# Four wo heads behind the cache stream, zero fills on ScalarE, MLP output in four partial sums, and TensorE's tail as a guarded last trip of its loop, in a one-core decode kernel

## The chip, the cores and the metric

Each kernel runs on one NeuronCore of a Trainium2 chip. The metric is device time in microseconds; "same" means within 2%. One execution of each kernel is profiled; the span on a profile page runs from the first to the last instruction, and the timed number is about 2 us above it.

## The reference

A decode step: attention over a K/V cache of 8192 positions (batch 4, 8 K/V heads, two query heads for each, head size 256), gated by the SiLU of an MLP.

```python
xn = layernorm(x)                                   # [4, 1, 448]
q  = xn @ wq                                        # 16 heads of 256
p  = softmax(q k^T * 256**-0.5)                     # k_cache [4, 8, 8192, 256], two q heads per k head
s  = (p v) @ wo                                     # v_cache [4, 8, 8192, 256], wo [4096, 448]
xn2 = layernorm(xn)
b  = xn + gelu(xn2 @ w3) @ w4                       # the rest of the MLP block is zero for S == 1
out = x + s * silu(b)
```

The caches are 268 MB of the 279 MB that must be read. There are 32 pairs of batch and K/V head; "K of head 2" below is the K cache (4 MiB) of the third pair in the order of work.

## The kernel before

SyncE issues every load, in order, on one queue. K and V have two buffers each.

```python
sp.dma_start(wq); sp.dma_start(w3); sp.dma_start(w4)        # into the two V buffers
load_k(0); load_k(1)
sp.dma_start(wo_sb[...], A_wo...).then_inc(S["dwo"], 16)    # all 16 heads, 3.5 MiB
for h in range(2, NH):
    load_k(h)            # waits until K of head h-2 has been transposed  (v_k)
    load_v(h - 2)        # waits until PV of head h-4 is done             (v_v)
load_v(NH - 2); load_v(NH - 1)                              # the last V in four pieces
```

```python
with nc.Fori(0, NH // 2, engines=[PE], head_slot={PE: 0}):
    body(0); body(1)
h = NH - 1
take(pe, "dwo", 16)
...                                        # wo of K/V heads 0 to 6, PV of head 30
for i in range(NPIECE):                    # V of head 31, piece by piece as it lands
    take(pe, "dvl%d" % i, 16)
    ... matmul(pst[1 + dh][:, 0:PVW], kn[...V piece...], pT[...])
take(pe, "v_ot")                           # VectorE scales the result
f_o(HKV - 1).then_inc(S["p_o"], 1)         # wo of the last K/V head: 16 matmuls
```

Then VectorE forms the output in two instructions and SyncE and ScalarE store it. The MLP output is 56 matmuls of 112 columns into one sum; GpSimd fills the parts of the V buffers that hold no weights with zeros (2,048 and 3,840 columns), because the first two passes of PV, both in the loop's first trip, multiply them by zero.

Of the kernel before, what the change touches and what calls it, by code (L numbers as in the profile page):

```python
# [32 lines left out]
def bass_recurrent_scan__gqa_block_cached__mixer_s_mlp__decode_kernel(  # L33
# [29 lines left out]
    assert D == NQD * DQ and Bn <= PQ  # L63
# [14 lines left out]
    CGW = P // NCG  # L78
    PV_PARTS = (0, 8, 16, 28, NCH)
    J_BC, J_TR, J_SUM = 1, 3, 8  # L80
    PVW = 32
    PIECES = (0, 32, 48, 56, NCH)
    NPIECE = len(PIECES) - 1

    x2d = A_x.rearrange("b s d -> b (s d)")
    out2d = out.rearrange("b s d -> b (s d)")

    with ExitStack() as es:
        def sb(name, shape, dty):
# [12 lines left out]
        OT = sb("OT", [P, HKV, REP, NHALF, Bn], BF16)  # L102
# [5 lines left out]
        sel = sb("sel", [P, REP], F32)  # L108
        po = sb("po", [P, DH], F32)
# [15 lines left out]
        xn4 = sb("xn4", [P, DQ], F32)  # L125
        res = sb("res", [P, DQ], F32)
# [3 lines left out]
        sg = sb("sg", [P, DQ], F32)  # L130
# [10 lines left out]
            + ["dvl%d" % i for i in range(NPIECE)]  # L141
            + ["p_td", "p_ta", "p_sc", "p_m1", "p_m2", "p_m3", "p_tr", "p_pv", "p_x", "p_q", "p_h", "p_h2", "p_o"]
            + ["v_ev", "a_ev", "v_rmax", "v_diag", "v_neg", "v_ot", "a_exp", "g_q", "g_c",
               "v_s", "v_k", "v_v", "v_po", "v_o", "g_o", "g_p", "g_f", "v_xT", "v_qT", "v_hT", "v_bout", "v_c", "v_w", "a_c", "v_out"])}
# [11 lines left out]
        q_ps = pst[1]  # L156
        h_ps = pst[2]
        h2_ps = pst[3]
        o_ps = pst[0]

# [7 lines left out]
        def prog_sp(sp):  # L168
# [10 lines left out]
            def load_k(h):  # L179
                b, g = divmod(h, HKV)  # L180
                if h >= 2:
                    sp.wait_ge(S["v_k"], h - 1)
                sp.dma_start(kn_dst(h), A_k_cache[b, g].rearrange("(p c) d -> p (c d)", p=P)
                             ).then_inc(S["dk%d" % (h % 2)], 16)

            def load_v(h):
                b, g = divmod(h, HKV)
# [5 lines left out]
                else:  # L193

                    sp.wait_ge(S["v_k"], h)
                    for i in range(NPIECE):
# [8 lines left out]
            sp.dma_start(wo_sb[:, :, :, :].rearrange("p h c n -> p h (c n)"),  # L205
                         A_wo.rearrange("(h p c) n -> p h (c n)", p=P, c=NHALF)
                         ).then_inc(S["dwo"], 16)
# [4 lines left out]
            load_v(NH - 1)  # L212
            sp.wait_ge(S["v_out"], 1)
# [6 lines left out]

        def prog_pool(gp):
            def put(h):
                b, g = divmod(h, HKV)
                gp.wait_ge(S["v_o"], h + 4)
                gp.tensor_copy(OT[:, g, :, :, b],
                               otmp[:, h % 2].rearrange("p dh r -> p r dh")
                               ).then_inc(S["g_p"], 1)
                gp.wait_ge(S["g_p"], h + 1)
                gp.sem_inc(S["g_o"], 1)
# [4 lines left out]
            c(gp.memset(ones_f[:, :], 1.0))  # L234
            c(gp.memset(pT[:, :, :].rearrange("p s n -> p (s n)"), 0.0))
            c(gp.memset(vflat[1][:, DK * HDH:NCH * DH], 0.0))
            c(gp.memset(vflat[0][:, DK * FH + NF * D:NCH * DH], 0.0))
            c(gp.memset(diag[:, :], 0.0))
            c(gp.memset(po[:, :], 0.0))
            c(gp.memset(rz[:, :, :].rearrange("p s r -> p (s r)"), 1.0))  # L240
            c.sync()
            for t in (ident_b, ident_f):
                c(gp.affine_select(out=t[:, :], in_=t[:, :], compare_op=ALU.not_equal, fill=1.0,  # L243
                                   base=0, pattern=[[-1, P]], channel_multiplier=1))
            gp.wait_ge(S["v_qT"], 1)
            for h in range(NH):
                b, g = divmod(h, HKV)
# [19 lines left out]
        def prog_act(act):  # L267
            act.dma_start(x_sb[:, :], x2d).then_inc(S["dx"], 16)
            c = _Chain(act, S["a_c"])
            for k, col in ((1, 0), (2, 8)):  # L270
                act.wait_ge(S["v_w"], k)
                c(act.activation(st[:, col + 2:col + 3], st[:, col + 1:col + 2], ACT.Sqrt))
            act.wait_ge(S["v_w"], 3)
            c(act.activation(gel_b[:, :], gel_a[:, :], ACT.Tanh))
            act.wait_ge(S["v_w"], 4)
            c(act.activation(sg[:, :], bout[:, :], ACT.Tanh, scale=0.5))
# [25 lines left out]
        def prog_dve(v):  # L302
# [34 lines left out]
            c(v.memset(psc[1][:, 0:NCH * REP], 0.0))  # L337
            c(v.memset(psv[:, 0:DH], 0.0))
            c.sync()
            v.sem_inc(S["v_diag"], 1)  # L340
            v.sem_inc(S["v_po"], 1)
            v.sem_inc(S["g_o"], 5)
            v.sem_inc(S["dv0"], 16)
            v.sem_inc(S["dv1"], 16)
            c(v.memset(h2_ps[:, 0:DQ], 0.0))
            for t in (x4, xn4):
                c(v.memset(t[:, :], 0.0))
# [7 lines left out]
            v.wait_ge(S["g_c"], 11)  # L355
            idv = ident_f[:, :].rearrange("p (m t) -> p t m", t=NHF)
            c(v.tensor_reduce(par[:, :], idv, AX.X, ALU.add))
            c(v.tensor_reduce(sel[:, :], ident_f[:, :].rearrange(
                "p (j r) -> p r j", j=NCG)[:, 0:REP], AX.X, ALU.add))
            c.sync()  # L360
            for k, dst in ((0, xnT), (1, xn2T)):
                v.wait_ge(S["p_x"], k + 1)

                for t in range(NHF):
                    for a in range(NHF):
# [3 lines left out]
                ins.then_inc(S["v_xT"], 1)  # L369
            v.wait_ge(S["p_q"], 1)  # L370
            c(v.tensor_copy(qT[:].rearrange("p b g dh hh -> p (b g dh hh)"),
                            q_ps[:, 0:NKC * Bn]))
            c.sync()
            v.sem_inc(S["v_qT"], 1)
# [10 lines left out]
            v.wait_ge(S["a_c"], 3)  # L385
# [5 lines left out]
            for src, dst in ((x_f, x4), (xn_f, xn4)):  # L391
                for i in range(NQD):
                    c(v.tensor_copy(dst[i * PQ:i * PQ + Bn, :], src[:, i * DQ:(i + 1) * DQ]))
            c.sync()
            v.wait_ge(S["p_h2"], 1)
            c(v.tensor_tensor(bout[:, :], h2_ps[:, 0:DQ], xn4[:, :], ALU.add))
            c.sync()
            v.sem_inc(S["v_w"], 1)
            v.sem_inc(S["v_bout"], 1)
            v.wait_ge(S["a_c"], 4)  # L400
            c(v.tensor_scalar(sg[:, :], sg[:, :], 1.0, 0.5, op0=ALU.add, op1=ALU.mult))
            c.sync()
            c(v.tensor_tensor(sg[:, :], sg[:, :], bout[:, :], ALU.mult))
# [18 lines left out]
            def f_rz(h):  # L422
                take(v, "p_m3")
                v.reciprocal(rz[:, h % 2, :], psm[:, P + REP:P + 2 * REP]
                             ).then_inc(S["v_s"], 1)
                take(v, "v_s")

            def f_po(h):
                take(v, "p_pv")
                v.sem_inc(S["v_v"], 1)  # L430
                v.tensor_copy(po[:, :], psv[:, 0:DH]).then_inc(S["v_po"], 1)  # L431

            ot_src = psv[:, DH:DH + NHALF * REP].rearrange("p (a r) -> p a r", a=NHALF)

            def f_ot(h, last=False):
                b, g = divmod(h, HKV)
                take(v, "p_tr")
                if not last:
                    take(v, "g_o")
# [5 lines left out]
                v.sem_inc(S["v_ot"], 1)  # L445
                v.sem_inc(S["v_o"], 1)

            with nc.Fori(0, NH // 2, engines=[mybir.EngineType.DVE]):
                for h in range(2):
                    for j in range(NGR):  # L450
# [4 lines left out]
                        if j == J_TR + 1:  # L455
                            f_ot(h - 3)
                        if j == J_SUM + 2:
                            f_rz(h - 1)
# [5 lines left out]
            f_negb(h)  # L464
            f_ot(h - 2, True)
            f_rz(h)
            f_po(h - 1)
            f_ot(h - 1, True)
            b, g = divmod(h, HKV)
            take(v, "p_pv")  # L470
            for dh in range(NHALF):
                ins = v.tensor_tensor(OT[:, g, :, dh, b], pst[1 + dh][:, 0:REP],
                                      rz[:, h % 2, :], ALU.mult)
            ins.then_inc(S["v_ot"], 1)
            v.wait_ge(S["p_o"], 1)
            c(v.tensor_tensor(res[:, :], o_ps[:, 0:DQ], sg[:, :], ALU.mult))  # L476
# [4 lines left out]
        def prog_pe(pe, xn_mark, xn2_mark):  # L481
            pe.wait_ge(S["g_c"], 11)
            for k, (src, mark) in enumerate(((xn_b, xn_mark), (xn2_b, xn2_mark))):
# [6 lines left out]
                if k == 0:  # L490
                    take(pe, "v_xT")
            take(pe, "dwq", 16)
            qo = q_ps[:, 0:NKC * Bn].rearrange("p (b a g dh hh) -> p g hh dh a b", b=Bn, a=NHF,
                                               dh=NHALF, hh=REP)
            for c in range(NQC):
                g, r = divmod(c, REP * NHALF)
                hh, dh = divmod(r, NHALF)
                for j in range(DK):
                    ins = pe.matmul(qo[:, g, hh, dh], wq_sb[:, j, c * P:(c + 1) * P],
                                    xnT[:, j], start=(j == 0), stop=(j == DK - 1))  # L500
# [8 lines left out]
            ins.then_inc(S["p_h"], 1)  # L509
            take(pe, "dw4", 16)  # L510
            take(pe, "v_hT")
            for k in range(NFK):
                for a in range(NHF):
                    for i in range(NQD):
                        ins = pe.matmul(h2_ps[i * PQ:i * PQ + Bn, 0:DQ], hT[:, k, a, :],
                                        w4_sb[:, a, k, i * DQ:(i + 1) * DQ],
                                        start=(k == 0 and a == 0),
                                        stop=(k == NFK - 1 and a == NHF - 1))
            ins.then_inc(S["p_h2"], 1)
            take(pe, "v_bout")  # L520
# [34 lines left out]
            def f_sum(h):  # L555
                take(pe, "a_exp")
                pe.matmul(psm[:, P + REP:P + 2 * REP], ones_f[:, :], rowsum[:, h % 2, :],  # L557
                          start=True, stop=True).then_inc(S["p_m3"], 1)

            def f_pv(h, lo, hi):  # L560
                if lo == 0:
                    take(pe, "v_ot")
                    take(pe, "dv%d" % (h % 2), 16)
                for kk in range(lo, hi):
                    o = kk % NCG * CGW
                    ins = pe.matmul(psv[o:o + REP, 0:DH],  # L566
                                    pT[:, h % 2, kk * REP:(kk + 1) * REP], vb[:, h % 2, kk, :],
                                    start=(kk < NCG), stop=(kk >= NCH - NCG))
                if hi == NCH:
                    ins.then_inc(S["p_pv"], 1)  # L570

            def f_tr(h):
                take(pe, "v_po")
                for dh in range(NHALF):
# [113 lines left out]
```

## Time and profile before

| | before |
|---|---|
| time, median of 3 runs | 660.26 us (659.96 to 661.8) |
| span of the profiled run | 658.7 us |
| bytes read | 279 MB |
| rate, 80 to 640 us | 428 to 436 GB/s in every 20 us |
| last bytes of the last V piece land | 654.15 us |
| output stores issued | 656.61 us |

These are lines of the page of the kernel before: the span; the rate of the loads in 40 equal slices of the span; the instruction queue (packets, MB, share of the DMA engines); and TensorE's transposes (count, then busy time, mean ns of one, idle time before them).

```profile
span 658.7 us, 25245 instructions
...
GB/s 363 433 410 427 427 432 430 434 434 430 432 432 430 432 434 430 434 432 434 428 434 428 432 432 436 430 432 436 426 434 430 436 430 434 434 426 436 426 426 223
...
q8 instruction: 10, 0.16, 0.1%
...
L528 PE MATMUL pst<-ident_b,kn 128*128 128x128 bf16 x4096 | 345.5, 238 | 101.2 <-PEq L219 99.7
```

The rate is flat but for the first and last slices: the kernel is its load stream. TensorE sat idle for 101 us ahead of the transposes, waiting for K. So nothing inside the loop can pay unless it keeps loads from being issued. Every 20 us window from 80 to 640 us reads 428 to 436 GB/s; whether a higher rate was to be had is not shown.

The timeline of SyncE (start us, issue us, what), kernel before:

```profile
43.85 0.33 SPq L183 DMA_DIRECT2D kn<-in_A_k_cache_dram  x1
51.57 0.33 SPq L191 DMA_DIRECT2D vb<-in_A_v_cache_dram  x1
64.95 0.33 SPq L183 DMA_DIRECT2D kn<-in_A_k_cache_dram  x1
71.49 0.33 SPq L191 DMA_DIRECT2D vb<-in_A_v_cache_dram  x1
82.61 0.33 SPq L183 DMA_DIRECT2D kn<-in_A_k_cache_dram  x1
86.54 0.33 SPq L191 DMA_DIRECT2D vb<-in_A_v_cache_dram  x1
```

These are K of head 2, V of head 0, K of head 3, V of head 1, K of head 4, V of head 2. A load adds 16 to its semaphore, and the trace has the time of each of the 16 increments, taken here as one for each of the core's 16 DMA engines. wo, ahead of K of head 2 in the queue, completes from 47.79 (first engine) to 50.23 (last): K of head 2 was issued 4 us before the first engine ran dry. V of head 1 completes from 86.71 to 89.07. From then on each 4 MiB follows the one before by 9.71 us.

The windows view (window, its length, then busy us and instruction count of PE, PEld, DVE, ACT and POOL, the granted TensorE clock, DMA share and GB/s), kernel before:

```profile
core 0: us, PE busy (x) PEld busy (x) DVE busy (x) ACT busy (x) POOL busy (x), PEclk, DMA share, GB/s
...
80.00:84.00 4.00, 4.00 (x108) 3.41 (x105) 2.11 (x5) 1.98 (x2) 0.00 (x0) 1.00 1.01 434
84.00:88.00 4.00, 3.95 (x91) 3.29 (x84) 2.04 (x6) 1.02 (x1) 0.19 (x1) 1.00 1.01 434
88.00:92.00 4.00, 4.00 (x96) 4.00 (x94) 2.05 (x6) 3.38 (x7) 0.00 (x0) 1.00 1.03 442
```

The end of TensorE's first trip, kernel before, from its timeline (start us, busy us, engine, line, operation, count, and in brackets the idle before it):

```profile
70.36 0.37 PE L548 MATMUL psm<-ident_f,rmax 128*2 128x128 f32 x1
70.52 1.91 PE L528 MATMUL pst<-ident_b,kn 128*128 128x128 bf16 x16
```

The last instruction of the trip and the first of the next follow each other. The end of the kernel before, from the timeline of all engines (start us, busy us, engine, line, operation, count, and in brackets the idle before it):

```profile
654.29 0.59 PE L630 MATMUL pst<-pT,kn 128*128 128x32 bf16 x16 [0.62 <-PEq L219]
655.03 0.23 DVE L472 TENSOR_TENSOR OT<-pst,rz 128x2 bf16<-128x2 f32 x2 [6.84 <-DVEq L219]
...
655.40 0.55 PE L610 MATMUL pst<-wo_sb,OT 128*4 128x112 bf16 x16 [0.53 <-PEq L219]
656.00 0.28 DVE L476 TENSOR_TENSOR res<-pst,sg 128x112 f32<-128x112 f32 x1 [0.74 <-PE pst L610]
656.31 0.28 DVE L478 TENSOR_TENSOR out_b<-res,x 128x112 bf16<-128x112 f32 x1
656.61 0.69 SPq L165 DMA_DIRECT2D out_dram<-out_b  x2
```

From the landing of the last V piece (654.15) to the store (656.61) is 2.46 us of strictly serial work.

### The profile page before, as it was taken

How to read it: one execution, taken by the hardware profiler on the slowest of the kernel's cores; microseconds unless marked ns; L12 is line 12 of the kernel's file. 1: busy time of each engine (PE TensorE's matmuls, PEld its weight loads, DVE VectorE, ACT ScalarE, POOL GpSimd, SP SyncE). 2: the span in 40 equal slices, each digit the busy share in tenths (PEclk: the TensorE clock that was granted, in tenths of full speed). 3: DMA queues.
4: the chain of work that ended last, by engine and by line, in shares of the span. 5: the costliest groups of instructions: out<-in, count | busy, mean ns of one | idle time of the engine just before them, and what ended most of it. 6: DMA issues, size and time to landing. Idle time of an engine off the chain costs nothing. (4 is left out here: it accounts for less than half of the span.)

```text
span 658.7 us, 25245 instructions
## 1 busy us (share of the span) xinstructions
PE 531.3 (81%) x11091; PEld 481.5 (73%) x11091; DVE 260.7 (40%) x585; ACT 252.6 (38%) x362; POOL 17.0 (3%) x76
## 2 busy tenths in 40 slices
PE   1489999896979879678887867987969698867895
PEld 1378888885969778577777756877858688866784
DVE  7234455242433424343433434442524343433440
ACT  1044444451434435234443423443524344423340
POOL 4000000000000000000000000000000000000000
PEclk9988799696797969798987979896979896978996
DMA  8999999999999999999999999999999999999995
GB/s 363 433 410 427 427 432 430 434 434 430 432 432 430 432 434 430 434 432 434 428 434 428 432 432 436 430 432 436 426 434 430 436 430 434 434 426 436 426 426 223
DMA packets 12324, 279.18 MB, mean 424 GB/s; under 512 B 1172, under 2 KB 3224, under 8 KB 3736
## 3 DMA queue, kind: packets, MB, share of 16 engines
q1 hardware_dynamic: 12288, 278.99, 98.9%
q8 instruction: 10, 0.16, 0.1%
q14 instruction: 2, 0.02, 0.0%
q10 hardware_dynamic: 24, 0.01, 0.0%
HBM read 278.99 MB, written 0.00 MB: 424 GB/s over the span
## 5 line engine op out<-in xcount | busy, mean ns | idle before, releaser
L528 PE MATMUL pst<-ident_b,kn 128*128 128x128 bf16 x4096 | 345.5, 238 | 101.2 <-PEq L219 99.7
L265 ACT ACTIVATE kT<-pst 128x1024 bf16<-128x1024 bf16 x224 | 229.4, 1024 | 361.7 <-ACTq L219 361.1
L528 PEld LDWEIGHTS pst<-ident_b,kn 128*128 128x128 bf16 x4096 | 277.6, 108 | 106.4 <-issue 105.8
L263 DVE COPY kT<-pst 128x1024 bf16<-128x1024 bf16 x288 | 197.8, 692 | 282.5 <-DVEq L219 282.3
L540 PE MATMUL psc<-qc,kT 128*128 128x2 bf16 x4096 | 179.2, 165 | 0.7 <-issue 0.7
L540 PEld LDWEIGHTS psc<-qc,kT 128*128 128x128 bf16 x4096 | 158.8, 98 | 22.8 <-issue 22.8
L566 PE MATMUL psv<-vb,pT 128*2 128x256 bf16 x2112 | 84.8, 284 | 2.5 <-issue 1.8
L566 PEld LDWEIGHTS psv<-vb,pT 128*2 128x2 bf16 x2112 | 39.8, 84 | 10.9 <-issue 2.8
L407 DVE TENSOR_REDUCE rmax<-psc 128x2 f32<-128x128 f32 x32 | 9.3, 292 | 49.4 <-DVEq L219 49.4
L576 PE MATMUL psv<-sel,po 128*128 128x2 f32 x136 | 25.1, 289 | 0.7 <-PEq L219 0.6
L576 PEld LDWEIGHTS psv<-sel,po 128*128 128x128 f32 x136 | 23.0, 237 | 0.9 <-issue 0.9
L284 ACT ACTIVATE pT<-psc,negb 128x64 bf16<-128x64 f32 x66 | 20.6, 332 | 5.2 <-ACTq L219 5.2
L412 DVE TENSOR_REDUCE gmax<-psm 2x1 f32<-2x128 f32 x32 | 8.9, 279 | 33.9 <-DVEq L219 33.9
L250 POOL COPY qc<-qT 128x4 bf16<-128x4 bf16 x32 | 5.9, 187 | 584.1 <-DVEq L430 574.5
L552 PEld LDWEIGHTS psm<-diag,ones_f 2*128 2x128 f32 x66 | 12.7, 239 | 6.0 <-issue 4.6
L552 PE MATMUL psm<-diag,ones_f 2*128 2x2 f32 x66 | 15.4, 301 | 1.1 <-PEq L219 0.9
L431 DVE COPY po<-psv 128x256 f32<-128x256 f32 x33 | 14.0, 425 | 4.8 <-DVEq L219 4.1
L284 ACT ACTIVATION_READ_ACCUMULATOR pT<-psc,negb 128x1 f32 x66 | 13.6, 206 | 0.0
L557 PE MATMUL psm<-rowsum,ones_f 128*128 128x2 f32 x66 | 12.4, 257 | 0.0
L486 PE MATMUL pst<-ident_b,xn_b 4*128 4x4 bf16 x14 | 0.6, 161 | 13.5 <-DVE xn_b L333 8.8
L486 PEld LDWEIGHTS pst<-ident_b,xn_b 4*128 4x128 bf16 x14 | 0.5, 100 | 13.6 <-POOL ident_f L243 8.8
L557 PEld LDWEIGHTS psm<-rowsum,ones_f 128*128 128x128 f32 x66 | 10.3, 196 | 0.2 <-issue 0.2
(77 smaller groups left out, 97.1 us busy)
## 6 DMA issues: line engine op xcount, KB each, us to landing
kn<-in_A_k_cache_dram SPq DMA_DIRECT2D x32, 4096.0 KB, 26.0
vb<-in_A_v_cache_dram SPq DMA_DIRECT2D x31, 4096.0 KB, 31.7
vb<-in_A_wq_dram SPq DMA_DIRECT2D x1, 3584.0 KB, 11.3
wo_sb<-in_A_wo_dram SPq DMA_DIRECT2D x1, 3584.0 KB, 46.9
vb<-in_B_w_dram SPq DMA_DIRECT2D x2, 1568.0 KB, 16.3
kn<-in_A_v_cache_dram SPq DMA_DIRECT2D x1, 2048.0 KB, 27.1
kn<-in_A_v_cache_dram SPq DMA_DIRECT2D x1, 1024.0 KB, 29.1
kn<-in_A_v_cache_dram SPq DMA_DIRECT2D x2, 512.0 KB, 30.2
```

Source lines behind the costliest of these rows:

```text
L263: engine.tensor_copy(dst, src).then_inc(S["v_ev"], 1)
L265: engine.activation(dst, src, ACT.Copy).then_inc(S["a_ev"], 1)
L284: ins = act.activation(pv_p[:, :, hh], sc[:, :, hh], ACT.Exp, bias=negb[:, s, hh:hh + 1], scale=SCALE, accum_out=rowsum[:, s, hh:hh + 1])
L407: v.tensor_reduce(rmax[:, :], psc[h % 2][:, 0:NCH * REP].rearrange("p (k h) -> p h k", h=REP), AX.X, ALU.max).then_inc(S["v_rmax"], 1)
L412: v.tensor_reduce(gmax[:, :], psm[0:REP, 0:P], AX.X, ALU.max).then_inc(S["v_s"], 1)
L431: v.tensor_copy(po[:, :], psv[:, 0:DH]).then_inc(S["v_po"], 1)
L528: ins = pe.transpose(dst[:, t * P:(t + 1) * P], kn[:, h % 2, GC * j + kl, half * P:(half + 1) * P], ident_b[:, :])
L540: ins = pe.matmul(psc[h % 2][:, kk * REP:(kk + 1) * REP], kT[:, j % RING, t * P:(t + 1) * P], qc[:, h % 2, half, :], start=(half == 0), st ...
L552: pe.matmul(psm[:, P:P + REP], ones_f[0:REP, :], diag[:, :], start=True, stop=True).then_inc(S["p_m2"], 1)
L557: pe.matmul(psm[:, P + REP:P + 2 * REP], ones_f[:, :], rowsum[:, h % 2, :], start=True, stop=True).then_inc(S["p_m3"], 1)
L566: ins = pe.matmul(psv[o:o + REP, 0:DH], pT[:, h % 2, kk * REP:(kk + 1) * REP], vb[:, h % 2, kk, :], start=(kk < NCG), stop=(kk >= NCH - NCG))
L576: ins = pe.matmul(psv[:, o:o + REP], po[:, dh:DH:NHALF], sel[:, :], start=True, stop=True)
```

## The change

Its intent: shorten that serial end by letting four heads of wo, which need no further attention work, land last; keep the code of the end from being fetched at the end, by making it a guarded last trip of the loop; and make the head of the program smaller and less dependent on GpSimd. The diff, cut to its core:

```diff
-            sp.dma_start(wo_sb[:, :, :, :]...).then_inc(S["dwo"], 16)
+            load_wo(NLATE, HQ, "dwo")                       # 12 heads; LATE = ((0, 1), (2,), (3,))
             for h in range(2, NH): load_k(h); load_v(h - 2)
             load_v(NH - 2); load_v(NH - 1)
+            for i, hs in enumerate(LATE):
+                load_wo(hs[0], hs[-1] + 1, "dwl%d" % i)     # 2 + 1 + 1 heads end the stream
 ... zero fills of the V buffers
-            c(gp.memset(vflat[1][:, DK * HDH:NCH * DH], 0.0))
-            c(gp.memset(vflat[0][:, DK * FH + NF * D:NCH * DH], 0.0))
+            for t in (vflat[1][:, DK * HDH:NCH * DH], vflat[0][:, DK * FH + NF * D:NCH * DH]):
+                c(act.activation(t, pT[:, 0, 0:1].broadcast_to([P, t.shape[1]]), ACT.Copy))
 ... MLP output; q and PV are widened in the same way (28 for 112, and 32 for 64 a head)
-                    for i in range(NQD):
-                        ins = pe.matmul(h2_ps[i * PQ:i * PQ + Bn, 0:DQ], hT[:, k, a, :],
-                                        w4_sb[:, a, k, i * DQ:(i + 1) * DQ], ...)
+                    o = i % NCG * CGW
+                    ins = pe.matmul(h2_ps[o:o + Bn, 0:D], hT[:, k, a, :], w4_sb[:, a, k, :], ...)
+            ...                                             # a copy, then four f32 matmuls add the sums
 ... TensorE's loop
-            with nc.Fori(0, NH // 2, engines=[PE], head_slot={PE: 0}):
-                body(0); body(1)
-            ...the tail...
+            with nc.Fori(0, NH // 2 + 1, engines=[e], head_slot={e: 64}) as it:
+                with pe.If(it != NH // 2):
+                    body(0)
+                    body(1)
+                with pe.If(it == NH // 2):
+                    finish()                                # the tail, ends with f_o of the late heads
```

The tail is rewritten too: wo of the early heads and the first pieces of the last V go into four partial sums each. The order of the batches is also reversed, and in a head the transposition of PV's result moves to the place of the row sums.

## The prediction

> **What bounds the kernel now.** The load stream: 429 to 436 GB/s in every 20 us stretch from 80 to 640 us (windows view); 279.2 MB at 434 GB/s is 643 of the 658.7 us span. TensorE waits 105 us for K (waits view), so compute inside the loop is worth nothing. What is left is the start and the end. The timeline's end: TensorE starts on the last V piece at 654.29 (0.59 us), VectorE scales until 655.26, 16 wo matmuls run 655.40 to 655.95, VectorE works until 656.59, the store lasts to 658.7.

> The last landing itself is late. By the trace's completion increments 15 of the 16 DMA engines finish the last V piece between 650.31 and 652.40, the sixteenth at 654.15. The instruction queue has a 16 KiB packet of 1.07 us at 644.15, just before one engine falls 1.8 us behind. [...] The code after the loop is fetched then, through the same DMA engines.

> **What the change does.**
> 1. Four of 16 wo heads (0.92 MB, about 2.3 us at the 385 GB/s of the wo load) move behind V. The bytes stay; V lands 2.3 us earlier, so its chain runs under the wo transfer. After the last landing 8 matmuls remain, about 0.3 us at the half clock of the tail (16 took 0.55). On the critical path: 1.66 us become 0.3; 1.3 us saved.
> 2. The tail becomes the loop's last trip, and TensorE's program shrinks from about 2530 to 1920 instructions (counted in the builds). All from the loop on should be fetched in the first trip, nothing at the end. Then the straggler goes and the stream ends near 652, not 654.15: 1.5 to 2 us saved.
> 3. Zero fills: 1.8 + 3.6 us of GpSimd become about 6 us of ScalarE (1024 columns take 1.02 us) between 10 and 17 us, before the Tanh at 20.9. Not critical: K of head 0 lands at 30.83.
> 4. q in 28 wide matmuls, not 112; MLP output in 14, not 56; PV in 32, not 64. The head is done at 24 us and waits for K anyway. Worth nothing.
> 5. Loop entry at slot 64 moves the fetch stalls of the first trip (2.1 us at 43.8, 1.5 at 59.4, 0.65 at 67.5). They matter only through the issue of the next loads. With wo shorter the queue runs dry 2.3 us earlier, near 45.5 on the fastest engine; K of head 2 was issued at 43.85, K of head 3 at 64.95, just in time. I expect at most a short dip on the faster engines, costing 0 to 0.7 us.

> **Predicted:** -1.3 - 1.8 + 0.2, about -3 us: 657.3 us, 8 in 10 between 655.6 and 659.4. Faster by over 2%: 0.01; within 2%: 0.98; slower: 0.01.

> **Signs.** Last V piece read near 650 to 651, last wo landing near 652 with increments within 2.2 us; no instruction packet after 100 us; store issued near 653.5; span near 655.7; loop stretches still 429 to 436 GB/s.

> **What would make it wrong.** The tail is fetched at the end after all [...]; starvation between 45 and 90 us above 1 us; TensorE at half clock is not through the other wo matmuls before the last landing; the straggler has another cause.

-1.3 - 1.8 + 0.2 is -2.8 us, its "about -3". The trace of the kernel before does show the packets: eight of 16 KiB from 20.43 to 72.22 us, none through the later trips of the loop, then two, at 644.15 and 651.46. The "half clock of the tail" is a granted clock of 0.50 from 650 us to the end.

## The result, and the profile after

| | before | after |
|---|---|---|
| time, median | 660.24 us (4 runs) | 660.73 us (4 runs, 660.33 to 661.85) |
| ratio, 95% interval | | 1.0005 (0.9985 to 1.0025), same |
| span of the profiled run | 658.7 us | 658.8 us |

A ratio is the mean time of one kernel's fast runs over that of the other's fast runs of the same rounds, so it is not quite the ratio of the medians. The expected 3 us did not come.

The page after, the same lines:

```profile
span 658.8 us, 22917 instructions
...
GB/s 363 441 382 424 432 366 444 418 444 430 430 444 416 446 414 446 424 436 440 420 442 418 444 418 442 436 426 440 420 444 416 444 428 434 434 426 442 418 429 296
...
q8 instruction: 7, 0.11, 0.1%
```

The last slice is fuller (296 for 223), as intended. But the third and the sixth slice have holes, 382 and 366 GB/s; the sixth covers 82 to 99 us. SyncE's issues after, in the timeline:

```profile
44.99 0.33 SPq L201 DMA_DIRECT2D kn<-in_A_k_cache_dram  x1
49.10 0.33 SPq L209 DMA_DIRECT2D vb<-in_A_v_cache_dram  x1
62.40 0.33 SPq L201 DMA_DIRECT2D kn<-in_A_k_cache_dram  x1
67.03 0.33 SPq L209 DMA_DIRECT2D vb<-in_A_v_cache_dram  x1
86.53 0.33 SPq L201 DMA_DIRECT2D kn<-in_A_k_cache_dram  x1
90.64 0.33 SPq L209 DMA_DIRECT2D vb<-in_A_v_cache_dram  x1
```

K of head 4 is issued at 86.53, 3.9 us later than before, although K of head 3 was issued 2.6 us earlier. By then the queue is running dry: V of head 1 completes from 85.60 (first engine) to 87.78 (last). The windows view after shows the hole:

```profile
core 0: us, PE busy (x) PEld busy (x) DVE busy (x) ACT busy (x) POOL busy (x), PEclk, DMA share, GB/s
...
80.00:84.00 4.00, 4.00 (x85) 4.00 (x83) 1.62 (x4) 2.20 (x3) 0.00 (x0) 1.00 0.95 410
84.00:88.00 4.00, 4.00 (x93) 3.21 (x90) 2.20 (x4) 1.90 (x2) 0.00 (x0) 1.00 0.80 279
88.00:92.00 4.00, 3.96 (x67) 2.81 (x61) 2.09 (x6) 1.02 (x1) 0.19 (x1) 1.00 0.82 352
```

Against 434 GB/s the two stretches miss 4 us x (155 + 82) GB/s, about 0.95 MB or 2.2 us of stream. What made K of head 4 late stands in TensorE's timeline after, at the end of its first trip:

```profile
66.01 0.27 PE L602 MATMUL psm<-ident_f,rmax 128*2 128x128 f32 x1
...
72.75 1.87 PE L582 MATMUL pst<-ident_b,kn 128*128 128x128 bf16 x16 [6.47 <-PEq L243]
```

TensorE idled 6.47 us, although K of head 2 had been there since 58.57. In between stands only the branch over the 404 instructions of the tail. These lines are from the views of its source line L739 (count, then shortest, median and longest in ns, first and last start; PEldq is TensorE's sequencer), in the first trip and in all later ones:

```profile
L739 PEldq COMPARE_BRANCH  x1: 6890/6890/6890, 65.1 to 65.1; - x1
...
L739 PEldq COMPARE_BRANCH  x16: 75/210/215, 104.1 to 640.2; - x16
```

The same branch takes 6.89 us the first time and 0.2 us later. The first sequencer instruction behind the jump runs at 72.02, and the instruction queue has a 16 KiB packet from 69.59 to 70.47. The transposes then run at a slow rate for a while (16 in 1.87 us, 1.06 us at 89.7); so they did at this place in the kernel before (1.91 us), without the idle. The end after, in the timeline of all engines:

```profile
653.51 0.56 PE L690 MATMUL pst<-pT,kn 128*128 128x32 bf16 x16
...
654.25 0.87 PE L680 MATMUL pst<-wo_sb,OT 128*32 128x112 bf16 x40 [0.17 <-PEq L243]
...
655.36 0.28 PE L680 MATMUL pst<-wo_sb,OT 128*32 128x112 bf16 x8 [0.24 <-PEq L243]
655.69 0.28 DVE L523 TENSOR_TENSOR res<-pst,sg 128x112 f32<-128x112 f32 x1 [1.29 <-PE pst L680]
656.00 0.27 DVE L525 TENSOR_TENSOR out_b<-res,x 128x112 bf16<-128x112 f32 x1
656.30 0.66 SPq L183 DMA_DIRECT2D out_dram<-out_b  x2
```

The serial end is what was planned: 1.08 us from the last landing (655.22) to the store. The stream itself ends later. The completion times of its last load, over the 16 DMA engines:

| | before: last V piece | after: last wo piece | difference |
|---|---|---|---|
| mean of 16 engines | 651.66 | 654.73 | +3.07 |
| slowest engine behind the mean | 2.49 | 0.49 | -2.00 |
| slowest engine | 654.15 | 655.22 | +1.07 |
| landing to store | 2.46 | 1.08 | -1.38 |
| store to end of span | 2.09 | 2.45 | +0.36 |
| span | 658.70 | 658.75 | +0.05 |

So two gains of 2.0 and 1.4 us are there, and 3.1 us of lost stream and 0.4 us at the very end take them back. But part of the 2.0 us came with the loss itself. In the kernel before, the slowest engine was 1.10 us behind the mean up to 641 us and 2.59 us behind right after the packet at 644.15, so that packet is worth about 1.4 of the 2.0 us. The other 0.6 us come from the hole at K of head 4: there the faster engines waited for the load, and the slowest engine's distance from the mean went from 1.30 to 0.29 us. Where the stream lost can be read from the steps between mean completions. From K of head 1 to K of head 2 the step was 19.45 us before and is 18.40; without the four late heads (which take 2.38 us at the end of the stream) it should be 17.07, so 1.33 us are lost. From V of head 1 to K of head 4 it is 11.92 instead of 9.71: 2.21 us lost. All other steps in this stretch are 9.7 to 9.95 in both; they and the earlier loads give back about 0.5 us.

The 0.36 us at the end lies in SyncE: its wait for the stores ends at 658.02 (658.33 before), and its next instruction comes 0.45 us later (0.16 before). No experiment asked why.

### The profile page after: what moved, and what is told of

It is laid out like the page before. It is cut to its first block, busy times and chain, and to the rows that moved or that the text cites. A ratio compares the mean times of both kernels' runs of the same rounds, so it can differ in the third digit from the quotient of the medians.

```text
span 658.8 us, 22917 instructions
## 1 busy us (share of the span) xinstructions
PE 550.9 (84%) x9941; PEld 474.2 (72%) x9941; DVE 274.3 (42%) x593; ACT 256.1 (39%) x364; POOL 13.6 (2%) x77
## 5 line engine op out<-in xcount | busy, mean ns | idle before, releaser
L582 PE MATMUL pst<-ident_b,kn 128*128 128x128 bf16 x4096 | 349.3, 240 | 84.9 <-PEq L243 84.9
L293 ACT ACTIVATE kT<-pst 128x1024 bf16<-128x1024 bf16 x224 | 229.3, 1024 | 364.5 <-ACTq L243 363.6
L594 PEld LDWEIGHTS psc<-qc,kT 128*128 128x128 bf16 x4096 | 158.2, 98 | 29.7 <-issue 29.2
L638 PE MATMUL psv<-vb,pT 128*4 128x512 bf16 x1056 | 86.0, 378 | 1.3 <-PEq L243 1.2
L612 PE MATMUL psm<-sel,po 128*128 128x2 f32 x272 | 36.6, 257 | 0.0
L612 PEld LDWEIGHTS psm<-sel,po 128*128 128x128 f32 x272 | 34.7, 196 | 0.0
L638 PEld LDWEIGHTS psv<-vb,pT 128*4 128x4 bf16 x1056 | 21.8, 82 | 16.7 <-issue 2.0
L469 DVE COPY po<-psv 128x512 f32<-128x512 f32 x34 | 23.5, 692 | 4.9 <-DVEq L243 4.1
L602 PEld LDWEIGHTS psm<-ident_f,rmax 128*2 128x2 f32 x32 | 2.6, 80 | 14.0 <-issue 14.0
## 6 DMA issues: line engine op xcount, KB each, us to landing
vb<-in_A_v_cache_dram SPq DMA_DIRECT2D x31, 4096.0 KB, 30.8
wo_sb<-in_A_wo_dram SPq DMA_DIRECT2D x1, 2688.0 KB, 43.8
```

The costliest lines, as they stand in the source:

```text
L293: engine.activation(dst, src, ACT.Copy).then_inc(S["a_ev"], 1)
L469: v.tensor_copy(po[:, slot], psv[:, 0:CP * DH]).then_inc(S["v_po"], 1)
L582: ins = pe.transpose(dst[:, t * P:(t + 1) * P], kn[:, h % 2, GC * j + kl, half * P:(half + 1) * P], ident_b[:, :])
L594: ins = pe.matmul(psc[h % 2][:, kk * REP:(kk + 1) * REP], kT[:, j % RING, t * P:(t + 1) * P], qc[:, h % 2, half, :], start=(half == 0), st ...
L612: ins = pe.matmul(dst(dh)[:, 0:width], po[:, slot, i * DH + dh:(i + 1) * DH:NHALF], sel[:, i, 0:width], start=(i == 0), stop=(i == CP - 1))
L638: ins = pe.matmul(psv[o:o + CP * REP, 0:CP * DH], pT[:, h % 2, kk * REP:(kk + CP) * REP], src[:, kk:kk + CP, :].rearrange("p c d -> p (c d)"),
```

## The experiments

The theory, called J in the expectations: the forward jump over the tail, at the end of the first trip, waits for the instruction block that holds the code behind the tail; K of head 4 is issued late for that; and since the head of the stream has lost four heads of wo, the queue has no cushion left. Rivals: the late wo, its small pieces, or the wider PV slow the stream as such; the loss is all at K of head 2; the comparison and the branch cost time, not the distance of the jump.

Each experiment ran beside the kernel before on the same chip. The first four shared 11 runs of it (median 660.25), the next four 11 others (660.66), the last four these and one more (12, 660.63). The two chips thus differ by 0.4 us, so compare small differences between e1 and e5 to e12 by the ratios. Each of their results was correct. In the table, "step" is the step in mean completion from V of head 1 to K of head 4 in the profiled run (9.71 is a full stream), and "landing" is the slowest completion of the last load.

| run | time, median (range) | ratio (95% interval) | K of head 4 issued | step | landing |
|---|---|---|---|---|---|
| after | 660.73 | 1.0005 (0.9985 to 1.0025) | 86.53 | 11.92 | 655.22 |
| e1 tail after the loop | 658.77 (658.25 to 659.05) | 0.9972 (0.9957 to 0.9987) | 75.69 | 9.71 | 652.60 |
| e2 tail first in the loop | 663.95 (663.3 to 664.92) | 1.0054 (1.0037 to 1.0071) | 82.41 | 9.71 | 657.07 |
| e3 all wo early | 661.42 (660.16 to 667.38) | 1.0015 (0.9992 to 1.0038) | 91.13 | 14.13 | 657.37 |
| e4 loop at slot 0 | 662.13 (661.25 to 662.87) | 1.002 (1.0003 to 1.0037) | 86.37 | 11.30 | 655.10 |
| e5 before, with late wo | 660.1 (659.25 to 664.57) | 0.9997 (0.9984 to 1.001) | 83.95 | 9.71 | 659.13 |
| e6 e1 with a long dummy jump | 662.58 (660.58 to 664.07) | 1.0025 (1.001 to 1.0041) | 84.68 | 11.13 | 655.02 |
| e7 e1 with a short dummy jump | 658.97 (658.31 to 660.26) | 0.9976 (0.9963 to 0.9988) | 77.47 | 9.71 | 653.37 |
| e8 e1 at slot 0 | 660.14 (658.94 to 662.3) | 0.9996 (0.9982 to 1.001) | 76.88 | 9.71 | 653.39 |
| e9 e1, fills on GpSimd | 659.26 (658.58 to 660.04) | 0.9982 (0.9967 to 0.9996) | 77.11 | 9.71 | 652.93 |
| e10 e1, MLP output as before | 660.03 (659.16 to 661.58) | 0.9994 (0.9979 to 1.0008) | 79.07 | 9.72 | 653.43 |
| e11 e1, two late heads | 659.43 (657.98 to 659.69) | 0.9975 (0.9961 to 0.999) | 79.25 | 9.71 | 652.33 |
| e12 e3 again, one look | 661.41 (1 run, unknown) | | 85.62 | 10.19 | 652.79 |

### e1: the tail after the loop again

```diff
-            with nc.Fori(0, NH // 2 + 1, engines=[e], head_slot={e: 64}) as it:
-                with pe.If(it != NH // 2):
-                    body(0)
-                    body(1)
-                with pe.If(it == NH // 2):
-                    finish()
+            with nc.Fori(0, NH // 2, engines=[e], head_slot={e: 64}):
+                body(0)
+                body(1)
+            finish()
```

> The changed kernel, but TensorE's tail stands after the loop again instead of as a guarded last trip. Theory J (the forward jump over the tail at the end of the first trip waits 6.5 us for its instruction block, K of head 4 is then issued at 86.5 us when the queue has run dry at 85.6 to 87.8, and the stream loses about 2 us): the idle of TensorE at 66 to 73 us shrinks below 2 us, K of head 4 is issued before 83 us, no DMA dip at 84 to 92 us, its slowest completion before 97.6 us (98.7 in the changed kernel). Instruction packets come back after 640 us and may put one engine behind by 1 to 2 us. Span 655.5 to 657.8, time 657.5 to 659.8. Rival R (the late wo pieces or the wider PV slow the stream as such, or the gap at K of head 2 is the whole loss): span stays 658.3 to 659.5.

Measured: 658.77 us, 1.96 us under the changed kernel, and clear of the kernel before (0.9957 to 0.9987). TensorE's timeline of this run at the end of the first trip:

```profile
63.86 0.27 PE L602 MATMUL psm<-ident_f,rmax 128*2 128x128 f32 x1
63.97 1.05 PE L582 MATMUL pst<-ident_b,kn 128*128 128x128 bf16 x16
```

No gap, and the fast rate (16 transposes in 1.05 us, in the changed kernel 1.87). K of head 4 is issued 10.8 us earlier than in the changed kernel, in SyncE's timeline of this run:

```profile
75.69 0.33 SPq L201 DMA_DIRECT2D kn<-in_A_k_cache_dram  x1
```

and the hole is gone in its windows view:

```profile
84.00:88.00 4.00, 4.00 (x87) 4.00 (x84) 1.63 (x4) 2.13 (x3) 0.00 (x0) 1.00 0.95 410
88.00:92.00 4.00, 4.00 (x94) 3.27 (x91) 2.25 (x5) 1.96 (x2) 0.00 (x0) 1.00 1.06 459
```

The mean of the last completions is 651.56, 3.17 us earlier than after and 0.1 earlier than before: the stream is whole. The late wo, the wide PV and the reversed batches are all still in this kernel, so together they do not slow the stream. The feared instruction packet near the end came at 652.84, after the last load, and harmed nothing: the program is 600 instructions shorter than before, and the packet before that one came at 95 us.

### e6 and e7: the jump by itself

Into e1 goes a guarded block at the end of the loop body that never runs: 200 transposes (about 400 instructions, as long as the tail) or 4 (8 instructions).

```diff
-            with nc.Fori(0, NH // 2, engines=[e], head_slot={e: 64}):
+            with nc.Fori(0, NH // 2, engines=[e], head_slot={e: 64}) as it:
                 body(0)
                 body(1)
+                with pe.If(it == NH // 2):
+                    for _ in range(200):                   # e7: range(4)
+                        pe.transpose(psm[0:REP, 0:P], rmax[:, :], ident_f[:, :])
             finish()
```

> The tail after the loop as in the first experiment, plus a guarded block of 200 never executed transposes (about 400 instructions, as many as the tail has) at the end of the loop body: it adds the jump of the changed kernel and nothing else. Theory J: TensorE idles 5 to 7 us again at the end of the first trip, K of head 4 is issued near 86 us, the dip at 84 to 92 us is back; span 658 to 660, 2 to 3.5 us over the first experiment's 656.2. If the gain of the first experiment came from something else than the removed jump, span 656 to 657.

> The same with 4 never executed transposes (8 instructions) in the guarded block: the comparison and the branch stay, but the jump goes only a few instructions ahead. Theory J: no idle above 1.5 us at the end of the first trip, K of head 4 issued before 80 us, span 655.8 to 657, time within 0.7 us of the first experiment's. If the comparison and the taken branch themselves are what costs, the idle of 5 to 7 us stays and the span is 658 to 660.

TensorE's timeline at the end of the first trip, with the long jump:

```profile
64.99 0.27 PE L602 MATMUL psm<-ident_f,rmax 128*2 128x128 f32 x1
70.87 1.87 PE L582 MATMUL pst<-ident_b,kn 128*128 128x128 bf16 x16 [5.61 <-PEq L243]
```

and with the short one:

```profile
65.65 0.27 PE L602 MATMUL psm<-ident_f,rmax 128*2 128x128 f32 x1
65.91 1.05 PE L582 MATMUL pst<-ident_b,kn 128*128 128x128 bf16 x16
```

The branch itself, from the views of L738 in e6 and then in e7:

```profile
L738 PEldq COMPARE_BRANCH  x1: 5957/5957/5957, 64.3 to 64.3; - x1
...
L738 PEldq COMPARE_BRANCH  x1: 334/334/334, 64.9 to 64.9; - x1
```

The comparison and the taken branch are there in both; the branch of e7 costs a few tenths (0.26 us from start to start, 0.11 in e1). Only the long jump idles, for 5.61 us. K of head 4 is then late, and the step is 11.13 us, 1.42 lost. The difference in time, 3.6 us, is not all of this kind: in e6 the stream ends 1.65 us later than in e7, and the rest is the end, where the longer program has an instruction packet at 653.97 and TensorE waits 1.04 us among its last matmuls, until 656.35. So the experiment shows the idle and the dry queue cleanly, the size of the time only roughly.

### e3 and e12: all of wo early, jump kept

```diff
             load_wo(NLATE, HQ, "dwo")
+            for i, hs in enumerate(LATE):
+                load_wo(hs[0], hs[-1] + 1, "dwl%d" % i)
 ...
-            for i, hs in enumerate(LATE):
-                load_wo(hs[0], hs[-1] + 1, "dwl%d" % i)
```

> The changed kernel with the last four wo heads loaded right after the other twelve, in the head of the stream; TensorE's program is the same, jump included. Theory J: the queue runs dry 2.3 us later, so K of head 2 (issued near 45) and K of head 4 (issued near 86.5, dry from 88) come in time or nearly so; no DMA dip at 84 to 92 us; the last V piece lands near 652.5 with a spread under 1 us; then the chain behind it is 1 to 2 us longer than in the changed kernel. Span 656.3 to 658, time 658.3 to 660. If starvation is not the cause, the last V piece lands near 655 as the last wo piece does now, and the span is above 659.5.

The expectation missed: 661.42 us. The profile fell on the slowest of six runs (667.38). In it TensorE idled 2.12 us until 45.19, inside the first body, waiting for nothing that the profile shows, at the place in the transposes where the same code crosses a block boundary in the changed kernel's trace (43.6 us, no stop there). K of head 2 came to be issued only at 47.12; four runs took 660.16 to 661.44, one 664.59.

> A second look at the third experiment (all wo in the head of the stream, tail as guarded last trip), whose profile fell on the slowest of its six runs: 667.4 us where four others took 660.2 to 661.4. In that profile TensorE lost 2.1 us to an instruction block at 43 us [...], so K of head 2 and head 4 were issued 2 and 4.6 us later than in the changed kernel. If that run was the odd one: K of head 4 issued near 86 to 88, mean step from V of head 1 to K of head 4 at most 11 us in place of 14.1, span 658 to 660. If the stalls are the rule with this order, span above 661.

What the timeline of e3 shows is that 18 matmuls of PV took 2.30 us from 49.95, in the changed kernel 1.24 us from 46.90.

In the second look, 661.41 us, the idle at the end of the first trip is there (start to start 6.85 us) and K of head 4 is issued at 85.62, but V of head 1 lasts until 86.80 to 88.73, and the step is 10.19: 0.48 us lost in place of 2.21. The last V piece lands at 652.79. This is the other half of the theory: the idle costs little as long as the four heads of wo are ahead of it in the queue. It rests on this one profile; in e3's, with the extra stop at 43 us, the same order lost 4.42 us at this step. The time is no better all the same, because the work behind the last V piece is longer in this arrangement: 4.14 us from landing to store in place of 1.08, more than the 1 to 2 us that I had allowed.

### e2: the tail first in the loop

```diff
             with nc.Fori(0, NH // 2 + 1, engines=[e], head_slot={e: 64}) as it:
+                with pe.If(it == NH // 2):
+                    finish()
                 with pe.If(it != NH // 2):
                     body(0)
                     body(1)
-                with pe.If(it == NH // 2):
-                    finish()
```

> The changed kernel with the guarded tail ahead of the two bodies in the loop, so that the first forward jump falls at about 24 us, where TensorE waits for K of head 0 until 30.8 anyway, and the tail's blocks are fetched by then. Theory J: no idle above 2 us at the end of the first trip, K of head 4 issued before 83 us, no instruction packet after 100 us, completions of the last wo piece within 1 us near 653, span 655.3 to 657, time 657.3 to 659. Rival R: span 658.3 to 659.5. If the tail's second block is only fetched in the last trip, the idle comes back near 640 us instead, with an instruction packet there.

Measured: 663.95 us, a miss by 5 us or more. The first jump did fall into the idle time before K of head 0, and the step at K of head 4 is 9.71. But TensorE now enters the body about 40 instructions ahead of the end of an instruction block, by count (64, and the 404 of the tail), and idles 2.82 us until 36.81, within the transposes of the first head. K of head 2 is issued at 48.48, when wo had completed from 45.31 to 47.15, and its step is 21.63, 4.2 us more than in e1. The hole moved from K of head 4 to K of head 2 and grew. That rival R also foresaw no gain does not support it: the loss is again a late issue.

### e4 and e8: the loop's entry at slot 0

```diff
-            with nc.Fori(..., head_slot={e: 64}) ...
+            with nc.Fori(..., head_slot={e: 0}) ...
```

> The changed kernel with the loop's entry at slot 0 of a fetch block in place of 64. The tail then begins near the end of one block and ends two blocks on, so one block is jumped over. Theory J with fetch on demand: the idle at the end of the first trip stays 5 to 7 us, the dip at 84 to 92 us stays, and the skipped block is fetched near 640 to 645 us, where TensorE idles another 2 to 7 us; span 658.5 to 664. If the slot does not matter: 658.8 like the changed kernel, no packet after 100 us.

> The first experiment with the loop's entry at slot 0 in place of 64. The fetch stalls of the first trip move: one within the first body's transposes would delay K of head 2 by up to 2.5 us, one behind them would not. If the slot matters it is by that: K of head 2 completes up to 1.5 us later on average and the span is 656.5 to 658.5; if it does not matter, span 655.8 to 656.8.

The stalls named in the two are estimates, from idles of TensorE already seen: 1.82 us (the kernel before, until 45.95) and 6.47 (the changed kernel's jump); for e8 also 2.12 (e3, until 45.19).

In e4 (the changed kernel at slot 0) the idle of the first trip is 6.46 us from start to start and the step is 11.30, near the changed kernel's 11.92. The block that I expected to be skipped was fetched in the first trip (eight packets, the last at 75.18), so no packet came near 640: that part of the expectation was wrong. Its last landing is 655.10, as in the changed kernel; the 1.4 us more in the time (1.9 in the span; the intervals of the ratios overlap) come after it, in a tail for which the granted TensorE clock was 0.50 from 644 to 652 us (1.00 and 0.57 in the changed kernel's profile). In e8 (e1 at slot 0) the profile's span, 656.9, is within the expected range, but the time is 660.14, 1.4 us over e1, with overlapping intervals. The timed number is 2.6 to 3.1 us above the span in five of its six runs (2.0 to 2.6 in e1), and in its profile an instruction packet runs at 659.31, after the last instruction. So slot 64 may be worth something up to 1 us; it is not settled.

### e5: the late wo alone, in the kernel before

```diff
-            sp.dma_start(wo_sb[:, :, :, :]...).then_inc(S["dwo"], 16)
+            load_wo(2 * REP, HQ, "dwo")
 ...
             load_v(NH - 1)
+            for g in range(2):
+                load_wo(g * REP, (g + 1) * REP, "dwl%d" % g)
 ...                                                     # TensorE: K/V heads 0 and 1 of wo come last
-            f_o(HKV - 1).then_inc(S["p_o"], 1)
+            f_o(HKV - 1)
+            for g in range(2):
+                take(pe, "dwl%d" % g, 16)
+                ins = f_o(g)
+            ins.then_inc(S["p_o"], 1)
```

> The kernel before with one part of the change alone: wo heads 0 to 3 end the load stream in two pieces, and their matmuls end TensorE's program. No jump inside the loop. Theory J: no gap at K of head 4; K of head 2 and K of head 3 were issued just in time before and are now up to 1.5 us late for the faster engines, so the stream ends 0 to 1 us later on average than 654.2; after the last landing 16 matmuls at half clock and VectorE remain, landing to store 1.3 us in place of 2.46. Instruction packets near 644 and 651 stay. Span 657.3 to 659, so at most 1.4 us gained. If the late wo by itself were the good part (its whole 1.3 us and no price), span 657.3 or less; if it were the bad part of the change, span above 659.5.

Measured: 660.1 us (ratio 0.9997), not told apart from the kernel before; the spans are 657.3, 658.1, 658.3, 658.3, 660.0 and 662.8 us, four of six in the expected range. The profile fell on the slowest. In it TensorE ran the first head's transposes at its slow rate until 45.9 us (8 of them in 1.01 us instead of 0.61); in the profile of the kernel before it was fast from 35.7 on. K of head 2 was issued at 48.01, after wo had completed, and 147 GB/s flowed from 46 to 50 us. At K of head 3 another 1.59 us were lost. What sets the rate is not shown: in these profiles the transposes begin at 29.7 to 31.4 us, and the fast rate set in between 34.6 us (e10) and 45.9 us (e5), 15 us after the start, while the granted clock of e5 read 1.00 in every window from 30 to 50 us. Either way, with wo late the stream has lost the cushion that would have hidden most of it.

### e9 and e10: the zero fills and the MLP output, each undone in e1

```diff
 e9:  +  c(gp.memset(t, 0.0)) for both parts, behind GpSimd's other fills; ScalarE's two copies dropped
 e10: +  the 56 matmuls of 112 columns into one sum; the copy and the four f32 sums dropped
```

> The first experiment (tail after the loop) with the zero fills of the two V buffers back on GpSimd, behind its other fills; TensorE waits for them ahead of the loop. They end near 10 us, the Tanh no longer waits behind 5.2 us of ScalarE copies, but K of head 0 lands at 30.5 either way. Expected: within 0.7 us of the first experiment (658.8 us), span 655.8 to 657. If the fills contend with the early loads, wq lands later than 12.1 us and the span grows by as much.

> The first experiment with the MLP output as before: 56 matmuls of 112 columns into one sum, no partial sums, no copy and no four f32 sums after them. The code before the loop grows by about 70 instructions and passes slot 64, so the loop's head falls into the next block, one more block is fetched in the head. Expected from the matmuls themselves: nothing, TensorE waits for K from 24 to 30.8 us anyway. Span 655.8 to 657.2; at most 1 us more if the extra instruction block lands on the slowest DMA engine or the stalls of the first trip move. A larger difference would say that the MLP form matters by more than its code size.

e9: 659.26 us (4 runs) against 658.77, within the expected 0.7. The fills are not on the critical path on either engine; wq completes at 12.04 in e9 and 12.24 in e1. e10: 660.03 us (4 runs), 1.26 over e1 in the medians, a little more than expected, with overlapping intervals (0.9979 to 1.0008 and 0.9957 to 0.9987). In its profile TensorE idles 0.97 us until 43.60 in the first trip, and K of head 2 is issued at 44.86 (43.98 in e1). Nothing shows the matmuls themselves; that the longer head shifts the blocks is a reading, not shown.

### e11: two late heads in place of four, in e1

```diff
-    LATE = ((0, 1), (2,), (3,))
+    LATE = ((0,), (1,))
```

> The first experiment with two late wo heads in place of four, one piece each. The queue in the head runs dry 1.2 us later, so K of head 2 (issued 44.0, first engine dry near 46.5) is in time: its mean completion is 9.71 us behind wo's, the stream ends up to 0.5 us earlier on average. The V chain has 1.2 us less cover at the end and may end after the last landing. Net: span 655.5 to 656.7, within 0.7 us of the first experiment.

659.43 us (4 runs), ratio 0.9975 against 0.9972: not told apart from e1. The mean of the last completions is 651.29, 0.27 us earlier than in e1, and the landing 652.33; but the store comes at 655.12, 2.8 us behind the landing. The V chain has lost its cover.

e1 has the best ratio of all versions: 0.28% faster than the kernel before (interval 0.13% to 0.43%); e7 and e11 are not told apart from it.

## Why the prediction was wrong

- **Late wo shortens the serial end: right.** -1.3 us predicted from landing to store, -1.38 measured. But the signs named with times all came about 3 us late: the last V piece is read from 653.51 (650 to 651 expected), wo lands at 655.22 (652), the store is issued at 656.30 (653.5).
- **Nothing is fetched at the end, the straggler goes: right in kind.** Seven instruction packets in place of ten, none after 77 us; the last piece completes over 0.74 us in place of 3.84, and its slowest engine is 2.0 us nearer to the mean. That this is close to the predicted 1.8 is in part luck: about 1.4 us of it is the missing fetch, the rest a by-product of the dry queue (e1, which never runs dry there, ends 1.04 us behind its mean and not 0.49). But "stream ends near 652, not 654.15" was wrong, since it took the mean of the stream as given: the mean moved by +3.07. The 2.0 us is also the profiled run's own: that run of the kernel before has a span of 658.7, while the median of the 11 that ran beside e1 is 658.1. In e1, where the stream is whole, the time gained is 1.5 us and not 3.
- **"I expect at most a short dip on the faster engines, costing 0 to 0.7 us": this is the step that failed.** It measured 3.5 us in the mean of the engines, 1.33 at K of head 2 and 2.21 at K of head 4. I had looked at K of heads 2 and 3, whose issue was just in time, and not at K of head 4, which had 4 us of cushion; and step 2, "all from the loop on should be fetched in the first trip", was written down as a gain without the price of that fetch. The price is 6.47 us of TensorE, since in the first trip the tail is jumped over and not run through. e1 takes the jump away and the 2.21 us are gone; e6 puts a jump of the same length back and 1.42 us are lost; e7 shows that a short jump costs nothing; e12 shows that the idle with wo still in the head costs 0.48. The loss at K of head 4 takes both parts of the change together.
- **How the jump comes to wait** is shown less far than that it waits. Counted in the trace from the stops at block boundaries, 256 instructions apart, the jump stands about 40 instructions into a block and lands in the very next one. TensorE entered the first of the two at 64.84, and the packet of the next came 4.75 us later, much as at the two boundaries before, crossed without a jump (4.53 and 4.94). So this may be the ordinary fetch of the next block, which the skipped instructions would else have covered; whether the branch itself starts a fetch, the runs do not tell. In e4 the target is two blocks on, and the branch takes no longer (6.12 us, 6.89 in the changed kernel).
- **The 1.33 us at K of head 2 is partly chance:** it was issued at 44.99, and between 43.98 and 44.66 in e1, e6, e7 and e9, whose loop code is the same up to there; in e1 0.34 us are lost at it. Two groups of transposes that still ran at the slow rate in the changed kernel's profile (until 37.2 us) make up 0.8 us of the lateness.
- **Zero fills and MLP worth nothing: consistent with e9 and e10**, within what these runs resolve.
- **Slot 64:** that the fetch stalls matter only through the issue of loads was right in these runs (e2 is the clearest case: 2.82 us of idle, K of head 2 issued 1.33 us after wo had completed, 4.2 us of step lost); which slot is best is not settled.
- The list of what could go wrong had "starvation between 45 and 90 us above 1 us", and that came.

## What to carry to other kernels

This kernel is bound by its load stream, and the change cost it time where the queue ran dry (1.33 us at K of head 2, 2.21 us at K of head 4). So before moving bytes to the end of a stream, list the issue time of every early load against the completion of the one ahead of it, and treat the difference as a budget that the move spends. Leave more than a microsecond of it: K of head 4 was issued 0.1 us before the first engine ran dry in e6 and still lost 1.42 us, 1.2 us before in e12 and lost 0.48; with 4 us, in the kernel before, nothing was lost. At the end of the loop's first trip the jump over some 400 instructions stopped TensorE for 5.6 to 6.9 us in four kernels here (the changed one, e4, e6, e12), the branch over 8 instructions took 0.33 us (e7): put rarely run code after the loop, or count such a wait at such a jump, at the moment when that engine sets the pace of the loads. When two gains that were each seen in the trace do not show in the time, compare the mean of the stream's completions and the spread around it separately; here one moved by +3.1 us and the other by -2.0.

## What else the traces show

- Fetches under the full load stream were not hidden: TensorE idled 1.82 us until 45.95 in the first trip of the kernel before, 6.47 us at the jump over 404 instructions. A packet takes 0.88 to 1.14 us, and in the four stalls that I could pair, TensorE went on about 2.5 us after the packet's start (43.41 and 45.95, 58.41 and 60.92, 65.63 and 68.14 before; 69.59 and 72.02 after).
- The changed kernel's loop of about 1,660 instructions of TensorE ran 17 trips on seven packets of 16 KiB, the last at 76 us.
- A delay on one DMA engine stayed: in the kernel before the 16 completions of one load were 2.3 us apart at 79 us and still 2.4 us apart at 623 us, and a dry queue (K of head 4 after: 0.5 us) drew them together. The slowest engine ended the stream, at 654.15 with the mean at 651.66.
- With one core at work 4 MiB came every 9.71 us, 432 GB/s, for over 500 us on end.
